# Recurrence of an RWKV-like layer before two expert layers: the mask, the token's own term and the scaled keys move between GpSimd, ScalarE, VectorE and TensorE

## The chip, the cores and the metric

The kernel runs on one core of one Trainium2 chip. The metric is the device time of one execution in microseconds. Before the change the median of three runs is 642.01 us (641.26 to 642.4).

## The reference, cut to what matters

```python
def _attn_ref(r, k, v, w, u):          # r, k, v: [4, 8, 768, 48]; w in 0.85 to 0.95; u: [8, 48]
    for t in range(S):
        cur = u * kt outer vt                       # the token's own term
        y[:, :, t] = rt . (state + cur)
        state = w * state + kt outer vt             # per batch and head: 48 x 48
def reference(...):
    x = attention output as [3072 tokens, 384]
    x = _moe_ref(x)      # tokens with a positive skip score: x + gate * expert(x); 8 experts, 384 -> 1024 -> 384
    return _moe2_ref(x)  # gate * expert(x) of the second layer
```

The time step loop is a recurrence per head; each token is then sent to one of eight experts in each of two layers. All is float32.

## The kernel before, in words

**Recurrence.** The 3072 tokens are 24 tiles of 128, six tiles for each of four batches; a tile has an even half (64 tokens) and an odd half. For a tile `n`, with powers of `w` in the tables TR, TK and TKH, the kernel makes the following pieces, each by a small function inside `attention()`:

- `prep_a`: KTL, the keys times TK (L530, on GpSimd), and XE, the queries times TR (L532, on VectorE), both [112 x 512]: the 48 channels of the odd half at partitions 0 to 47 and those of the even half at 64 to 111. `prep_b` copies the odd half's queries to XO on ScalarE.
- `amat`: TensorE multiplies keys and queries of a half into `a_ps` (L575, L576; 16 products, each of which stands twice in the trace, as two passes of float32). ScalarE copies the result back to XE and XO (L578), and GpSimd zeroes the part in which the key is not before the query, with two `affine_select` (L581).
- `prep_rk` and `prep_kq`: the token's own term. `rkt` = query times key (L547; on GpSimd in 16 tiles, on VectorE in the 8 of RKV), times `u` (L557), summed over the 48 channels of a head into `q` (L562), and `qv` = `q` times the values (L566). In the same function the scaled keys KDE (L560) and KDO (L564) for the state products are made. All of these are VectorE's.
- `uy`: state products `up` (L597, L599) between output products `yp` (L604, L606) on TensorE. ScalarE brings the new state back (L612, L614).
- `finish`: VectorE adds `yp` and `qv` into `xall` (L617), which frees the one bank that `yp` has.

The order on each engine is the order of the code (`manual_schedule`). An iteration `n` of the loop issues: `uy` for the even state of `n` and the odd output of `n-1`; `finish(n-1)`; `prep_a(n+3)`; `amat(n+2)`; `prep_kq(n+2)`; the loads of later tiles, on SyncE (RK for two tiles, `kr` with keys and queries by token, values); `uy` for the odd state and the even output of `n`; `gate_l`, `gate_x` (gate logits of finished tiles, by TensorE); from `n` = 6 on a scatter of a finished tile's rows by GpSimd (L273). `tick` places one operation of the gating of four tiles (`route`) at a time among these.

**Experts.** After the last tile the first expert runs in plain float32, then 16 more jobs of matrix products, in which TensorE is fed from weights that arrive from memory during the job before.

PSUM has eight banks: `a` twice, `y`, `ue`, `uo` in the recurrence, and three for gating.

Of the kernel before, what the change touches and what calls it, by code (L numbers as in the profile page):

```python
# [19 lines left out]
C = 64  # L20
# [23 lines left out]
# slots of a job at which a piece of the next weights is split, and blocks of the next rows are transposed, by the job's row tiles  # L44
# [8 lines left out]
W_LO, W_HI = 0.25, 1.5  # L53
# row tiles that are gated together, by their first: how many, and after how many slots
# [130 lines left out]
def attn_moe_moe_kernel(ctx: ExitStack, tc: tile.TileContext, t, out):  # L185
# [96 lines left out]
    def route(lt, X, g0, n, two, idx_out, ec):  # L282
        """lt: [96, n * 128] parts of the logits; X: row tiles; ec: which first slots.  Yields the engine of the operation to come."""
# [75 lines left out]
    def start(g, lag=0, burst=False, mult=1):  # L359
        """one at a time: they share a bank and the counts"""  # L360
# [5 lines left out]
    def tick(kind, now=False, burst=False):  # L366
        """the next operation of the gating under way if it waits for this engine; after another engine's, some slots later"""
# [37 lines left out]
    def attention():  # L405
        with ExitStack() as actx:
# [6 lines left out]
            u_b = cst.tile([128, DM], F32, name="u_b")  # L413
# [11 lines left out]
            KTL = [cst.tile([128, H, C], F32, name=f"KTL{i}") for i in range(NX)]  # L425
            NL = 3
# [14 lines left out]
            def load_kr(hb):  # L441
                kr[hb] = tok_p.tile([128, LT, 2, DM], F32, tag="kr", bufs=3, name="kr")
                nc.sync.dma_start(out=kr[hb], in_=t["kr"][hb * LT * 128:(hb + 1) * LT * 128].rearrange("(a p) k c -> p a k c", p=128))
# [803 lines left out]
```

## Time and profile before

| | |
|---|---|
| median of 3 runs | 642.01 us |
| span of the profiled execution | 648.0 us |
| recurrence up to the first expert's first product | about 190 us |
| busy: TensorE, VectorE, ScalarE, GpSimd | 87%, 63%, 46%, 46% |
| VectorE in the recurrence | 95% and more of most slices |
| mean granted TensorE clock | 0.928 |

The page names engines PE (TensorE), PEld (its weight loads), DVE (VectorE), ACT (ScalarE), POOL (GpSimd) and SP (SyncE). The times of the profiled execution are about 6 us longer than the median of the runs. The busy share of the whole span mixes the recurrence, in which VectorE hardly rests, with the experts, in which TensorE hardly rests; so stages are read apart.

### The profile page before, as it was taken

What the parts mean: (1) busy time and instruction counts of PE and PEld (TensorE: products, weight loads), DVE (VectorE), ACT (ScalarE), POOL (GpSimd) and SP (SyncE); (2) the same over time, 40 slices, a digit from 0 to 9 for tenths busy, and PEclk for the clock granted to TensorE, in tenths of its full rate; (3) what the DMA queues carried; (4) which work ended last, traced back from release to release, by engine and by line L of the source; (5) the groups of instructions that cost most, each with busy time, mean ns of one, the idle gap of its engine ahead of it and who ended that gap; (6) DMA issues with size and microseconds to landing.
All of it is one profiled execution on the core that took longest, in us unless ns stands there. A gap on an engine that the chain in (4) does not pass through costs nothing. (4 is left out here: it accounts for less than half of the span.)

```text
span 648.0 us, 13115 instructions
## 1 busy us (share of the span) xinstructions
PE 562.8 (87%) x5186; PEld 501.0 (77%) x5188; DVE 405.8 (63%) x732; ACT 295.4 (46%) x584; POOL 298.7 (46%) x312
## 2 busy tenths in 40 slices
PE   5796678778789989999999999997979979699993
PEld 3585566666667888898988999986869868599993
DVE  7998999999725467756676535436454464655320
ACT  5664455564425545554455426443424334254320
POOL 7765585776623175655323224644272524523201
PEclk8877888887979999999999999997998989799997
DMA  8985988679162987676665436342323434333000
GB/s 184 241 203 151 280 213 216 154 171 351 56 220 83 303 277 226 203 243 189 197 183 167 149 105 193 127 148 98 126 79 122 154 105 131 104 127 109 35 13 26
DMA packets 51896, 104.69 MB, mean 162 GB/s; under 512 B 5724, under 2 KB 37592, under 8 KB 51824
## 3 DMA queue, kind: packets, MB, share of 16 engines
q1 hardware_dynamic: 44016, 89.15, 47.7%
q0 software_dynamic: 5904, 11.82, 5.0%
q10 hardware_dynamic: 1904, 2.78, 1.7%
q8 instruction: 43, 0.70, 0.5%
q14 instruction: 29, 0.24, 0.1%
HBM read 82.98 MB, written 26.96 MB: 170 GB/s over the span
## 5 line engine op out<-in xcount | busy, mean ns | idle before, releaser
L1039 PE MATMUL g<-xh,w1h 128*128 128x256 f32 (+3 forms) x384 | 126.4, 329 | 19.1 <-ACT hr L1044 19.1
L1039 PE MATMUL g<-xh,w1l 128*128 128x256 f32 (+3 forms) x384 | 122.8, 320 | 0.0
L1039 PE MATMUL g<-xl,w1h 128*128 128x256 f32 (+3 forms) x384 | 122.4, 319 | 0.0
L1041 DVE SCALAR_TENSOR_TENSOR hl<-g,hh 128x256 fp32r<-128x256 f32 (+1 forms) x128 | 61.2, 480 | 93.1 <-ACT hh L1040 92.5
L1063 PE MATMUL g<-w2h,hh 128*128 128x384 f32 x312 | 109.2, 350 | 0.0
L1063 PE MATMUL g<-w2h,hl 128*128 128x384 f32 x312 | 105.5, 338 | 0.0
L1063 PE MATMUL g<-w2l,hh 128*128 128x384 f32 x312 | 105.2, 337 | 0.0
L1039 PEld LDWEIGHTS g<-xh,w1h 128*128 128x128 f32 x384 | 74.4, 194 | 25.4 <-ACT hr L1044 20.5
L1040 ACT ACTIVATE hh<-g 128x256 fp32r<-128x256 f32 (+1 forms) x128 | 55.1, 430 | 70.1 <-PE g L1039 68.8
L860 POOL TENSOR_TENSOR w1l<-s,w1h 128x1024 fp32r<-128x1024 f32 x14 | 33.4, 2389 | 114.1 <-ACT w1h L859 69.0
L1039 PEld LDWEIGHTS g<-xl,w1h 128*128 128x128 f32 x384 | 74.4, 194 | 1.8 <-DVE xl L1021 0.2
L1039 PEld LDWEIGHTS g<-xh,w1l 128*128 128x128 f32 x384 | 74.2, 193 | 1.6
L860 DVE TENSOR_TENSOR w1l<-s,w1h 128x1024 fp32r<-128x1024 f32 x28 | 57.6, 2056 | 20.9 <-ACT w1h L859 20.9
L273 POOL DMA_INDIRECT xs<-xall,idx_all x48 | 52.3, 1089 | 38.0 <-DVE cum L351 15.9
L273 POOL DMA_INDIRECT out<-rows,ids x30 | 29.2, 973 | 87.3 <-ACT rows L894 62.4
L1063 PEld LDWEIGHTS g<-w2h,hh 128*128 128x128 f32 x312 | 59.3, 190 | 3.1 <-issue 3.0
L1021 DVE TENSOR_TENSOR xl<-xt_ps,xh 128x256 fp32r<-128x256 f32 (+3 forms) x48 | 23.7, 495 | 57.3 <-ACT xh L1020 53.4
L1063 PEld LDWEIGHTS g<-w2l,hh 128*128 128x128 f32 x312 | 58.9, 189 | 0.1
L1063 PEld LDWEIGHTS g<-w2h,hl 128*128 128x128 f32 x312 | 58.5, 188 | 0.0
L606 PE MATMUL yp<-VSE,XE 112*64 112x48 f32 x384 | 31.5, 243 | 26.7 <-DVE xall L617 25.2
L606 PEld LDWEIGHTS yp<-VSE,XE 112*64 112x64 f32 x384 | 28.3, 157 | 28.6 <-DVE xall L617 26.9
L860 DVE TENSOR_TENSOR w2l<-s,w2h 128x1152 fp32r<-128x1152 f32 x28 | 37.9, 1354 | 14.0 <-ACT w2h L859 13.5
(194 smaller groups left out, 1207.2 us busy)
## 6 DMA issues: line engine op xcount, KB each, us to landing
s<-in_w1b SPq DMA_DIRECT2D x24, 512.0 KB
s<-in_w1a SPq DMA_DIRECT2D x21, 512.0 KB
RK<-in_rk SPq DMA_DIRECT2D x24, 384.0 KB
kr<-in_kr SPq DMA_DIRECT2D x12, 768.0 KB
s<-in_w2b SPq DMA_DIRECT2D x16, 576.0 KB
s<-in_w2a SPq DMA_DIRECT2D x14, 576.0 KB
xs<-zrow SPq DMA_DIRECT2D x5, 970.0 KB
VSE<-in_v SPq DMA_DIRECT2D x12, 384.0 KB
```

The costliest lines, as they stand in the source:

```text
L273: i = P.indirect_dma_start(out=dst, out_offset=bass.IndirectOffsetOnAxis(ap=idx_col, axis=0), in_=src, in_offset=None, bounds_check=last, ...
L606: T.matmul(y_ps[ny][0:64, h, 0:D], lhsT=XE[x][0:112, h], rhs=VSE[iy][0:112, jy, h], start=True, stop=True)
L860: (P if j in POOL_LO else V).tensor_tensor(out=lo, in0=x, in1=hi.bitcast(F32), op=ALU.subtract)
L1021: V.tensor_tensor(out=lo, in0=tp[:, 0:cap], in1=hi.bitcast(F32), op=ALU.subtract)
L1039: T.matmul(p, lhsT=a[:, kb, f], rhs=b[:, kb], start=(kb == 0 and i == 0), stop=(kb == KB - 1 and i == 2))
L1040: A.activation(out=hh[:, fb], in_=p[:, 0:full], func=ACTF.Relu)
L1041: V.scalar_tensor_tensor(out=hl[:, fb], in0=p[:, 0:full], scalar=0.0, in1=hh[:, fb].bitcast(F32), op0=ALU.max, op1=ALU.subtract)
L1063: T.matmul(p, lhsT=a[:, fb, r], rhs=b[:, fb], start=(fb == 0 and x == 0), stop=(fb == FB - 1 and x == 2))
```

## The change

Six edits in the recurrence, and what follows from them in other places:

1. KTL is made by VectorE (it was GpSimd's).
2. GpSimd makes one product per tile: RKP = query times key in the channel layout, [112 x 512].
3. TensorE sums the token's own term: 16 products with RKP as the stationary operand and one column of `u` per head as the moving one, into a bank of its own, `q_ps`, right behind the products of `amat`.
4. The mask is a product: VectorE multiplies `a_ps` in PSUM by `before` (ones where the key is before the query) into XE and XO. ScalarE's copies and GpSimd's `affine_select` are gone.
5. `prep_kq` keeps KDE, KDO and `qv`; `qv` reads `q_ps` in PSUM. `rkt`, its product with `u` and the reduction are gone; the queries by token are no longer loaded (`kr` is half as large).
6. `ue` and `uo` become one bank `u`, which pays for the bank of `q_ps`. `u` is loaded by channel (`u_c`, two loads) rather than spread over all partitions. The lower bound on the square of `w` below which the general path is taken rises from 0.25 to 0.7.

```diff
-W_LO, W_HI = 0.25, 1.5
+W_LO, W_HI = 0.7, 1.5
-RKV = (0, 1, 2) + tuple(range(7, NT, 4))
...
-            u_b = cst.tile([128, DM], F32, name="u_b")
+            u_c = cst.tile([112, H], F32, name="u_c")
+            before = cst.tile([128, 1, C], F32, name="before")
...
+            RKP = [cst.tile([112, H, C], F32, name=f"RKP{i}") for i in range(NX)]
...
-                kr[hb] = tok_p.tile([128, LT, 2, DM], F32, tag="kr", bufs=3, name="kr")
+                kr[hb] = tok_p.tile([128, LT, DM], F32, tag="kr", bufs=3, name="kr")
...
+                P.memset(before, 1.0)
+                for r0 in (0, 64):
+                    P.affine_select(out=before[r0:r0 + 64], in_=before[r0:r0 + 64], pattern=[[0, 1], [1, C]], compare_op=ALU.is_gt, fill=0.0, base=0, channel_multiplier=-1)
                 for r0 in (0, 64):
                     nc.sync.dma_start(out=w_c[r0:r0 + D], in_=t["wT"].unsqueeze(2))
+                    nc.sync.dma_start(out=u_c[r0:r0 + D], in_=t["u"].rearrange("(h d) -> d h", d=D))
...
             def prep_a(n):
...
-                P.tensor_tensor(out=kt_[0:112], in0=RK[i][:, 1, j], in1=TK, op=ALU.mult)
+                P.tensor_tensor(out=RKP[x], in0=RK[i][:, 0, j], in1=RK[i][:, 1, j], op=ALU.mult)
+                V.tensor_tensor(out=kt_[0:112], in0=RK[i][:, 1, j], in1=TK, op=ALU.mult)
...
-            def prep_rk(n):
...
             def prep_kq(n):
-                V.tensor_tensor(out=rk, in0=rk, in1=u_b, op=ALU.mult)
                 tick("dve")
                 tick("dve")
...
-                V.tensor_reduce(out=q, in_=rk.rearrange("p (h d) -> p h d", d=D), axis=AX.X, op=ALU.add)
...
-                V.tensor_tensor(out=qv, in0=VSE[hb % NL][:, j], in1=q.to_broadcast([128, H, D]), op=ALU.mult)
+                V.tensor_tensor(out=qv, in0=VSE[hb % NL][:, j], in1=q_ps.pop(n).to_broadcast([128, H, D]), op=ALU.mult)
...
             def amat(n):
...
+                q_ps[n] = ps.tile([128, H, 1], F32, tag="q", name="q_ps")
+                for h in range(H):
+                    for r0, o in ((64, 0), (0, 64)):
+                        T.matmul(q_ps[n][o:o + 64, h], lhsT=RKP[x][r0:r0 + D, h], rhs=u_c[r0:r0 + D, h:h + 1], start=True, stop=True)
                 for X, r0 in ((XE[x], 0), (XO[x], 64)):
-                    A.copy(out=fl(X[r0:r0 + 64]), in_=fl(a_ps[r0:r0 + 64]))
-                # keys before the query; below partition 64 all of the odd buffer stays
-                for X, n_, base in ((XE[x], 64, 0), (XO[x], 128, 64)):
-                    P.affine_select(out=X[0:n_], in_=X[0:n_], pattern=[[0, H], [1, C]], compare_op=ALU.is_gt, fill=0.0, base=base, channel_multiplier=-1)
+                    V.tensor_tensor(out=X[r0:r0 + 64], in0=a_ps[r0:r0 + 64], in1=before[r0:r0 + 64].to_broadcast([64, H, C]), op=ALU.mult)
+                    tick("dve")
...
-                    up = ps.tile([128, H, D], F32, tag="uo" if uodd else "ue", name="up")
+                    up = ps.tile([128, H, D], F32, tag="u", name="up")
...
-            nc.sync.dma_start(out=u_b, in_=t["u"].partition_broadcast(128))
```

**Order on VectorE**, one iteration of the loop without gating in it, from one `finish` (`xall`) to the next; first before, then now. The numbers behind a name are buffers; L532 is L539 in the new numbering, L560 L555, L564 L558, L566 L563, L617 L616.

```order
L617 TENSOR_TENSOR xall<-yp,qv 128x384
L532 TENSOR_TENSOR XE_127<-RK_139,TR 112x512
L557 TENSOR_TENSOR rkt<-rkt,u_b 128x384
L560 TENSOR_TENSOR KDE_122<-kr,TKH 64x384
L562 TENSOR_REDUCE q<-rkt 128x8
L564 TENSOR_TENSOR KDO_125<-kr,TKH 64x384
L566 TENSOR_TENSOR qv<-VSE_141,q 128x384
L617 TENSOR_TENSOR xall<-yp,qv 128x384
```

```order
L616 TENSOR_TENSOR xall<-yp,qv 128x384
L537 TENSOR_TENSOR KTL_136<-RK_144,TK 112x512
L539 TENSOR_TENSOR XE_128<-RK_144,TR 112x512
L579 TENSOR_TENSOR XE_131<-a_ps,before 64x512
L579 TENSOR_TENSOR XO_135<-a_ps,before 64x512
L555 TENSOR_TENSOR KDE_123<-kr,TKH 64x384
L558 TENSOR_TENSOR KDO_126<-kr,TKH 64x384
L563 TENSOR_TENSOR qv<-VSE_146,q_ps 128x384
L616 TENSOR_TENSOR xall<-yp,qv 128x384
```

Two operations are gone between two `finish` (the product with `u` and the reduction), and three are new: KTL ahead of XE, and the two masks, which stand where the product with `u` stood.

**Order on GpSimd**, one iteration in the loop's later part, from one scatter of rows (L273, now L272) to the next; first before, then two iterations now.

```order
L273 DMA xs_76<-xall,idx_all 2048x388
L530 TENSOR_TENSOR KTL_136<-RK_139,TK 112x512
L547 TENSOR_TENSOR rkt<-kr 128x384
L581 AFFINE_SELECT XE_127<-XE_127 64x512
L581 AFFINE_SELECT XO_131<-XO_131 128x512
L273 DMA xs_76<-xall,idx_all 2048x388
```

```order
L272 DMA xs_76<-xall,idx_all 2048x388
L536 TENSOR_TENSOR RKP_141<-RK_144 112x512
L272 DMA xs_76<-xall,idx_all 2048x388
L536 TENSOR_TENSOR RKP_142<-RK_145 112x512
L272 DMA xs_76<-xall,idx_all 2048x388
```

Of four operations between two scatters one is left, and it waits for a load alone, no longer for ScalarE.

**Order on SyncE**, the first loads of the program, which the first operation of the recurrence waits for; first before, then now.

```order
L453 DMA w_c<-in_wT 48x8 x2
L439 DMA RK_139<-in_rk 48x2x1024 x2
L680 DMA RK_139<-in_rk 16x2x1024
L443 DMA kr<-in_kr 128x2x768
L682 DMA u_b<-in_u 128x384
L448 DMA VSE_141<-in_v 128x2x384
```

```order
L458 DMA w_c<-in_wT 48x8
L459 DMA u_c<-in_u 48x8x1
L458 DMA w_c<-in_wT 48x8
L459 DMA u_c<-in_u 48x8x1
L440 DMA RK_144<-in_rk 48x2x1024 x2
L679 DMA RK_144<-in_rk 16x2x1024
L444 DMA kr<-in_kr 128x2x384
L449 DMA VSE_146<-in_v 128x2x384
```

Two loads of `u_c` with single elements now stand ahead of the first RK; `u_b` behind it is gone and `kr` has half the columns.

## Rows read from the trace of the kernel before

**Rows 1.** Busy time by engine in four stretches; the first row names the columns.

```profile
core 0: us, PE busy (x) PEld busy (x) DVE busy (x) ACT busy (x) POOL busy (x), PEclk, DMA share, GB/s
...
32.29:169.04 136.75, 105.61 (x2134) 89.08 (x2134) 132.35 (x212) 74.29 (x149) 87.57 (x118) 0.84 0.79 208
...
189.60:648.00 458.40, 419.87 (x2588) 386.14 (x2585) 238.07 (x434) 196.71 (x388) 177.79 (x144) 0.97 0.46 144
...
13.00:14.00 1.00, 1.00 (x24) 1.00 (x20) 0.97 (x2) 0.96 (x2) 1.00 (x1) 0.50 1.09 184
...
59.85:76.92 17.07, 12.43 (x293) 10.37 (x291) 16.58 (x24) 9.96 (x21) 11.40 (x11) 1.00 1.04 252
```

**Rows 2.** Timeline of VectorE: start us, duration us, engine, line, operation, operands.

```profile
36.15 0.55 DVE L557 TENSOR_TENSOR rkt<-rkt,u_b 128x384 f32<-128x384 f32 x1
36.62 0.54 DVE L560 TENSOR_TENSOR KDE<-kr,TKH 64x384 f32<-64x384 f32 x1
37.09 0.54 DVE L562 TENSOR_REDUCE q<-rkt 128x8 f32<-128x384 f32 x1
37.66 0.56 DVE L564 TENSOR_TENSOR KDO<-kr,TKH 64x384 f32<-64x384 f32 x1
...
39.19 0.68 DVE L532 TENSOR_TENSOR XE<-RK,TR 112x512 f32<-112x512 f32 x1
39.79 0.55 DVE L557 TENSOR_TENSOR rkt<-rkt,u_b 128x384 f32<-128x384 f32 x1
...
62.80 3.24 DVE L564 TENSOR_TENSOR KDO<-kr,TKH 64x384 f32<-64x384 f32 x1
```

**Rows 3.** Timeline of GpSimd beside the last row above.

```profile
62.78 0.65 POOL L581 TENSOR_SCALAR_AFFINE_SELECT XO<-XO 128x512 f32<-128x512 f32 x1
63.41 1.26 POOL L530 TENSOR_TENSOR KTL<-RK,TK 112x512 f32<-112x512 f32 x1
64.63 0.99 POOL L547 TENSOR_TENSOR rkt<-kr 128x384 f32<-128x384 f32 x1
```

**Rows 4.** VectorE's groups in 32.29 to 169 us: busy us, mean ns | idle.

```profile
L564 DVE TENSOR_TENSOR KDO<-kr,TKH 64x384 f32<-64x384 f32 x20 | 33.5, 1677 | 0.6
L532 DVE TENSOR_TENSOR XE<-RK,TR 112x512 f32<-112x512 f32 x20 | 22.1, 1106 | 0.0
L560 DVE TENSOR_TENSOR KDE<-kr,TKH 64x384 f32<-64x384 f32 x20 | 19.4, 971 | 0.0
...
L306 DVE TENSOR_SCALAR eq<-lg 128x4 f32<-128x4 f32 x4 | 2.8, 710 | 0.0
```

**Rows 5.** Two lines of VectorE, whole span: ns min/median/max, first and last start.

```profile
L617 DVE TENSOR_TENSOR xall<-yp,qv x24: 542/550/558, 32.3 to 185.4; 128x384 f32<-128x384 f32 x24
...
L562 DVE TENSOR_REDUCE q<-rkt x24: 533/535/540, 17.7 to 170.6; 128x8 f32<-128x384 f32 x24
```

**Rows 6.** Who waited for whom, 32 to 187 us: total us, times, longest.

```profile
PE yp L606 <- DVE xall L617: 25.2, 12, 6.2
```

**Rows 7.** Timeline of TensorE: around 12 us, and around 60 us.

```profile
12.28 0.37 PE L575 MATMUL a_ps<-XE,KTL 64*64 64x64 f32 x1 [5.20 <-POOL KTL L530]
...
14.18 1.08 PE L512 MATMUL tps<-ident,TH 48*128 48x48 f32 x8
...
60.11 0.27 PE L575 MATMUL a_ps<-XE,KTL 64*64 64x64 f32 x1
...
61.19 0.24 PE L597 MATMUL up<-VSO,KDO 128*48 128x48 f32 x1
...
64.15 0.27 PE L575 MATMUL a_ps<-XE,KTL 64*64 64x64 f32 x1
```

**Rows 8.** Timeline of SyncE's queue: its first issues, with their time.

```profile
0.98 0.88 SPq L453 DMA_DIRECT2D w_c<-in_wT  x2
```

**Rows 9.** Timeline of VectorE: its first wait.

```profile
10.41 0.69 DVE L532 TENSOR_TENSOR XE<-RK,TR 112x512 f32<-112x512 f32 x1 [3.45 <-DMA RK<-in_rk]
```

**Rows 10.** The page, DMA queues: packets, MB, share of 16 engines' span.

```profile
q1 hardware_dynamic: 44016, 89.15, 47.7%
```

More of the change, by code (lines that the diff above doesn't have):

```diff
@@ L441, in load_kr @@
             def load_kr(hb):
-                kr[hb] = tok_p.tile([128, LT, 2, DM], F32, tag="kr", bufs=3, name="kr")
-                nc.sync.dma_start(out=kr[hb], in_=t["kr"][hb * LT * 128:(hb + 1) * LT * 128].rearrange("(a p) k c -> p a k c", p=128))
+                kr[hb] = tok_p.tile([128, LT, DM], F32, tag="kr", bufs=3, name="kr")
+                nc.sync.dma_start(out=kr[hb], in_=t["kr"][hb * LT * 128:(hb + 1) * LT * 128].rearrange("(a p) c -> p a c", p=128))
             def load_v(hb, a=0, b=LT):
@@ L521, in setup5 @@
                     A.copy(out=X[i][r0:r0 + D], in_=X[0][r0:r0 + D])
-            qv_t, q_t, ktil, rk_t = {}, {}, {}, {}
+            ktil, qv_t, q_ps = {}, {}, {}
             def prep_a(n):
@@ L542, in zero_state @@
                 A.copy(out=fl(VSE[n // LT % NL][64:112, n % LT]), in_=warm_src[64:112, 0:DM])
-            def prep_rk(n):
-                hb, j = n // LT, n % LT
-                rk = wk.tile([128, DM], F32, tag="rkt", bufs=3, name="rkt")
-                (V if n in RKV else P).tensor_tensor(out=rk, in0=kr[hb][:, j, 1], in1=kr[hb][:, j, 0], op=ALU.mult)
-                rk_t[n] = rk
             def prep_kq(n):
@@ L553, in prep_kq @@
                 b = n % NB
-                rk = rk_t.pop(n)
-                q = wk.tile([128, H, 1], F32, tag="q", name="q")
-                qv = wk.tile([128, H, D], F32, tag="qv", bufs=3, name="qv")
-                V.tensor_tensor(out=rk, in0=rk, in1=u_b, op=ALU.mult)
+                V.tensor_tensor(out=fl(KDE[b][0:64]), in0=kr[hb][0:64, j], in1=TKH[0:64], op=ALU.mult)
                 tick("dve")
                 tick("dve")
-                V.tensor_tensor(out=fl(KDE[b][0:64]), in0=kr[hb][0:64, j, 0], in1=TKH[0:64], op=ALU.mult)
+                V.tensor_tensor(out=fl(KDO[b][64:128]), in0=kr[hb][64:128, j], in1=TKH[64:128], op=ALU.mult)
                 tick("dve")
-                V.tensor_reduce(out=q, in_=rk.rearrange("p (h d) -> p h d", d=D), axis=AX.X, op=ALU.add)
                 tick("dve")
-                V.tensor_tensor(out=fl(KDO[b][64:128]), in0=kr[hb][64:128, j, 0], in1=TKH[64:128], op=ALU.mult)
-                tick("dve")
-                V.tensor_tensor(out=qv, in0=VSE[hb % NL][:, j], in1=q.to_broadcast([128, H, D]), op=ALU.mult)
+                qv = wk.tile([128, H, D], F32, tag="qv", bufs=3, name="qv")
+                V.tensor_tensor(out=qv, in0=VSE[hb % NL][:, j], in1=q_ps.pop(n).to_broadcast([128, H, D]), op=ALU.mult)
                 tick("dve")
@@ L703, in attention @@
             prep_v(0)
-            prep_rk(0)
             prep_kq(0)
@@ L711, in attention @@
             prep_b(2)
-            prep_rk(1)
             prep_kq(1)
-            prep_rk(2)
             load_rk(2)
@@ L735, in attention @@
                     prep_a(n + 3)
-                    prep_rk(n + 3)
                 tick("dve")
@@ L783, in bank @@
             def bank(tag):
-                return ps.tile([128, H, D], F32, tag=tag, name="f_ps").rearrange("p h d -> p (h d)")
+                return ps.tile([128, H, D], F32, tag=tag, bufs=2 if tag == "a" else 1, name="f_ps").rearrange("p h d -> p (h d)")
             uy(None, 1, NT - 1, 0)
@@ L798, in attention @@
             gate_l(NT - 2)
-            first_T(bank("uo"), (0, 1), 0, CAPA)
-            first_T(bank("ue"), (2,), 0, CAPA)
+            first_T(bank("u"), (0, 1), 0, CAPA)
+            first_T(bank("a"), (2,), 0, CAPA)
             gate_x(NT - 1)
```

2 lines of the change are left out of this document (1 added, 1 removed).

## The prediction

> **What bounds the kernel now.** I read the stretches first. Between the first and the last of 20 equal steps of the recurrence, 32.29 to 169.04 us, VectorE is busy for 132.35 of 136.75 us, GpSimd for 87.57 and TensorE for 105.61 at a granted clock of 0.84; after 189.6 us TensorE takes over, busy for 419.87 of 458.40 us at 0.97 [rows 1]. The list of waits says who holds whom in the recurrence: TensorE's output products wait 25.2 us in 12 waits for VectorE's `finish`, which frees their only bank [rows 6]. So VectorE's list of operations per tile is the step, 136.75 / 20 = 6.84 us.
>
> That list is not slow by its work. In a tile without hindrance one round, from a product with `u` at 36.15 to the next at 39.79, is 3.64 us: `u` 0.47, KDE 0.47, the reduction 0.57, KDO with `qv` and `finish` 1.53, XE 0.60 [rows 2]. Another KDO, the same 64 x 384, takes 3.24 us, from 62.80 to 66.04, while GpSimd runs three operations without a gap from 62.78 to 65.62, which read SBUF [rows 2, 3]. In the groups this is the rule: KDO, XE and KDE take 33.5, 22.1 and 19.4 us for 20 each, where 20 free ones would be 11.2, 13.6 and 10.8; that is 39.4 us of standing still, 1.97 us per step, and even a comparison of four elements averages 0.71 [rows 2, 4]. Two lines never suffer: `finish`, with one input in PSUM, is 0.542 to 0.558 us in all 24 tiles, and the reduction, with one input, 0.533 to 0.540 [rows 5]. So VectorE stands still when it reads two tensors from SBUF while GpSimd works there. The step is 3.64 work + 1.97 standing still of these three + 1.23 rest (gating, the 5 of 20 `rkt` made here, the stalls of short operations, a little idle).
>
> The Trainium skill, page "SBUF — State Buffer", section "Who interferes with whom", has the same division (two SBUF inputs contend with a GpSimd operation that reads SBUF, one does not), but has the lock end with the instruction that holds it. The KDO row differs: it outlasted three. By the page alone one product of GpSimd costs at most its own length; by the rows a queue of them costs its whole length.
>
> **The change part by part.**
>
> VectorE's work. Out: the product with `u`, 0.47, and the reduction, 0.57 [rows 2]. In: KTL, of XE's shape, 0.60, and two masks of 64 x 512. No row shows a mask; it has XE's columns, and a PSUM input costs `finish` nothing (0.55 for 384 columns, as KDE's 0.54 from SBUF), so 0.60 is the lower bound; a change of the starting partition costs 0.1 (the reduction's step ahead of KDO is 0.57 for a duration of 0.54, KDE's 0.47), so 0.78 is the upper bound, XE's whole free duration of 0.68 and that change, nothing overlapped [rows 2, 5]. I take 0.70, XE's step and the change, since steps overlap so in every row. 3.64 - 1.04 + 0.60 + 1.40 = 4.60 us. The rest, 1.23, loses 0.12 (5 x 0.47 / 20) and most of the short operations' stalls; I take 0.75, between 0.6 and 1.1. Without GpSimd: 5.35.
>
> GpSimd's share. Of KTL 1.26, `rkt` 0.99 and two selections of 0.65, 3.55 us per tile, one product of KTL's kind is left, 1.26 [rows 3]. Before, 3.55 us of it held the three long operations for 1.97, a ratio of 0.55; applied to 1.26 that is 0.70. Lower bound nothing, if the product always falls beside the masks, `qv` or `finish`, which now all have one input in PSUM (4 of 8 operations); upper bound its own length, 1.26, since a scatter now stands between two products. I take 0.75. Step: 5.35 + 0.75 = 6.10, against 6.84; 20 steps: -14.8 us. With all lower ends 4.40 + 0.6 + 0 = 5.0, with all upper ones 4.76 + 1.1 + 1.26 = 7.1: -37 to +5 us; the low end is cut by TensorE, next.
>
> TensorE. Around 60 us, at a clock of 1.00, a whole tile went through without a wait from 60.11 to 64.15: 4.04 us, of which the 32 passes of `amat` are 1.08 [rows 1, 7]. The 16 new products are 32 passes too, with the same 48 or 64 rows and 64 columns of weights but one moving column where `amat` has 64. No row has them. Below, half of `amat`, 0.5 us, if only the loads count; above, `amat` at half clock, 14.18 - 12.28 = 1.9 [rows 1, 7]. I take 0.93, near `amat`, because the weights are the same size. TensorE then needs 5.0 and some 0.4 for hand-overs, 5.4 per tile at full clock: it stays behind VectorE's 6.1, with little room. The wait of `q_ps` for the last `qv` (one bank) holds TensorE until just before `finish`, for which the next output products wait anyway; behind it in TensorE's queue stand these first. The state's one bank adds nothing: the odd product reads the even state's copy, and so waits for it already.
>
> ScalarE loses two copies per tile; it was busy for 74.29 of 136.75 us [rows 1], and what they fed is used two tiles later: nothing. As for loads, 4.7 MB of `kr` go; DMA was at a share of 0.79 in this stretch [rows 1] and no wait of VectorE's for it is in it: nothing.
>
> At the start VectorE waits for RK until 10.41 [rows 9]. Ahead of it now stand two loads of `u_c` of 384 single elements each. At the issue they cost 2 x 0.44, as `w_c` [rows 8]; a packet in the main queue takes 0.477 x 16 x 648 / 44016 = 0.112 us of one engine [rows 10], so 768 of them over 16 engines 5.4 us at most. I take +1.3, near the issue's row. From 10.41 to the first `finish`, 21.9 us later [rows 5, 9], four KTL and six masks come, 2.4 + 4.2, and three products with `u`, reductions and `rkt` go, 3 x 1.51: +2.1 of work. At the step's prices three tiles and a fourth XE with their tables are some 13 us of work, an estimate, so 9 stood still; with one product of GpSimd per tile rather than four I take half of that back, -4.5, and give 0.4 for the first scaled keys, which now wait for TensorE's sums at half clock. That is -2.0, with the load -0.7, and 3 either way.
>
> After 169 us, VectorE no longer sets the step, and after 189.6 TensorE, 92% busy, sets the time [rows 1]: what the recurrence saves moves all that follows ahead unchanged.
>
> The sum: -14.8 - 0.7 = -15.5: 648.0 becomes 632.5 in the profile. The median of the runs is 6.0 below the profile's span; the same difference gives **626.5 us**.
>
> **The rivals.**
>
> Nearly no standing still (faster still). For it: RKP waits only for its load, and four of eight operations of VectorE no longer fight it. Then VectorE needs 5.35 and TensorE's 5.4 is the step: 20 x 1.44 = -28.8 and the start's -0.7: 612.5. Against it: KTL with XE, and KDE with KDO, are still 2.2 us of two-input work per step, and GpSimd is freer to meet them.
>
> TensorE at a mixed clock (a smaller gain). Its clock was 0.84 in this stretch; if it stays there and the new products cost `amat`'s 1.08, (4.04 + 1.08) / 0.84 + 0.4 = 6.5 per step: -6.8 and -0.7, 634.5. For it: VectorE's stalls leave gaps, after which the rows at half clock come. Against: fuller work; at 60 to 77 us, with 12.43 of 17.07 busy, it was 1.00 [rows 1].
>
> The new products cost full price on TensorE (slower). Place: between `amat` and the next output products, in every tile. Price: `amat`'s half-clock 1.9 us; at the clock of 0.84, (4.04 + 1.9) / 0.84 + 0.4 = 7.5 per step, 20 x 0.63 = +12.6, with the start 654. It decides against the change from (4.04 + x) / 0.84 + 0.4 = 6.84 on, so x = 1.37 us, 43 ns per pass. For it: 32 more loads of weights for one column each. Against: `amat`, with the same weights, needs 34 ns per pass at full clock. The Trainium skill, "TensorE: Matmul & The Clock Gate", section "LDWEIGHTS (loading the stationary operand)", speaks for this rival: a load costs its columns / 1.2 ns, however few columns move; for 64 that is 53 ns, an estimate of 1.7 us for 32 in a row. `amat`'s passes, 34 ns apart, show loads that overlap between the two halves of the array, and I expect the same here.
>
> The lock stays what it was (no change). If VectorE's long pairs meet GpSimd's product every time, the step is 5.35 + 1.26 + 0.2 = 6.8: 642 with the start. For it: the KDO row, which stood for the whole of what GpSimd had. Against: that was three operations of 2.90 us, now it is one of 1.26 with a scatter behind it [rows 3].
>
> That the general path is taken does not happen: `w` is at least 0.85, its square 0.7225, above the new bound.
>
> **How the numbers follow.** Forecast 0.48 (621 to 632); nearly no standing still 0.22 (607 to 619); mixed clock 0.11; full price 0.11; the lock as before 0.08, of which a third on either side and a third within 0.2%, which is about what a measurement of this kernel can tell from no change. Faster: 0.48 + 0.22 + 0.11 + 0.03 = 0.84, rounded down to 0.83; same 0.03, rounded up to 0.04; slower 0.11 + 0.03, 0.13 after that. The range leaves out the full price and the lowest part of the second case: 610 to 641.
>
> **What would show it.** Right: KDO, KDE, XE and KTL near 0.55 to 0.7 us in the median with outliers of at most some 1.9, masks and `qv` never stretched, 20 steps in about 122 us, RKP alone on GpSimd at 1.3, 32 `q_ps` passes in about 0.9 us, TensorE's waits for `finish` shorter. Wrong: masks over 1 us, or stretched; `q_ps` passes over 43 ns apart with VectorE waiting for TensorE at `finish`; RK's first load landing after 14 us; outliers of 3 us on VectorE as before.

## The result, and the profile after

The changed kernel takes 650.46 us (median of 4 runs, 646.81 to 651.38) against 641.63 of the kernel before beside it: ratio 1.0128, 95% interval 1.0093 to 1.0163. Slower by 1.3%, where 2.4% faster was forecast. Twice more it was 1.0159 (1.0092 to 1.0226) and 1.0148 (1.0109 to 1.0188). The kernel before took 640 to 642 us on some chips and 648 to 649 on others, so all that follows goes by ratios of runs on one chip.

The stretches of the changed kernel are 20 steps from the first `finish`, a stretch at half clock, and the experts; they answer to [rows 1].

```profile
core 0: us, PE busy (x) PEld busy (x) DVE busy (x) ACT busy (x) POOL busy (x), PEclk, DMA share, GB/s
35.96:174.56 138.60, 124.61 (x2781) 109.36 (x2783) 116.29 (x226) 51.75 (x108) 37.68 (x30) 0.83 0.71 176
155.70:169.40 13.70, 13.30 (x191) 10.96 (x190) 9.33 (x23) 4.58 (x11) 2.31 (x2) 0.50 0.90 301
190.00:648.30 458.30, 418.35 (x2583) 384.99 (x2582) 236.73 (x431) 196.83 (x387) 179.05 (x145) 0.97 0.47 146
```

20 steps take 138.60 us, not the 122 forecast and not less than the 136.75 of before. VectorE, which had been busy for 132.35 us of them, is busy for 116.29; TensorE went from 105.61 to 124.61 at the same clock. The two engines have changed places. The second row is the longest stretch at half clock (1.2 GHz) behind the first `finish`; TensorE hardly rests in it. The third row, the experts, is as before. The list of waits, which answers to [rows 6], says so too (who waited for whom: us in total, times, longest):

```profile
DVE xall L616 <- PE yp L603: 23.3, 12, 4.2
...
PE up L598 <- ACT VSE L611: 3.1, 2, 1.7
PE q_ps L577 <- issue: 2.4, 2, 1.6
PE a_ps L572 <- issue: 2.3, 2, 1.9
PE up L598 <- issue: 2.2, 1, 2.2
```

The output products' wait for `finish`, 25.2 us before, is gone from TensorE's list; `finish` now waits 23.3 us for the output products. VectorE's groups in 36 to 174.6 us (busy us, mean ns | idle), against [rows 4]:

```profile
L537 DVE TENSOR_TENSOR KTL<-RK,TK 112x512 f32<-112x512 f32 x20 | 16.0, 802 | 0.0
L555 DVE TENSOR_TENSOR KDE<-kr,TKH 64x384 f32<-64x384 f32 x20 | 15.5, 773 | 0.2
L539 DVE TENSOR_TENSOR XE<-RK,TR 112x512 f32<-112x512 f32 x20 | 14.7, 736 | 0.0
L558 DVE TENSOR_TENSOR KDO<-kr,TKH 64x384 f32<-64x384 f32 x20 | 14.1, 703 | 0.3
L579 DVE TENSOR_TENSOR XO<-a_ps,before 64x512 f32<-64x512 f32 x20 | 13.9, 695 | 0.3
L579 DVE TENSOR_TENSOR XE<-a_ps,before 64x512 f32<-64x512 f32 x20 | 13.4, 670 | 0.7 <-PE a_ps L573 0.6
L616 DVE TENSOR_TENSOR xall<-yp,qv 128x384 f32<-128x384 f32 x21 | 11.6, 553 | 19.7 <-PE yp L603 19.7
```

With free durations (0.68, 0.54, 0.68 and 0.56 us, [rows 2]) the first four groups, with two inputs from SBUF, would be 49.2 us; they are 60.3, so 11 us of standing still are left of 39.4, although KTL has joined them. TensorE's timeline (start, duration, operands, count, idle before) has the new products once with a hole, then at half clock (73.29), then at full clock (81.84):

```profile
37.37 0.23 PE L577 MATMUL q_ps<-u_c,RKP 48*64 48x1 f32 x4
39.15 1.31 PE L577 MATMUL q_ps<-u_c,RKP 48*64 48x1 f32 x28 [1.55 <-issue]
...
73.29 1.82 PE L577 MATMUL q_ps<-u_c,RKP 48*64 48x1 f32 x32
75.03 0.32 PE L596 MATMUL up<-VSO,KDO 128*48 128x48 f32 x1
...
81.84 1.05 PE L577 MATMUL q_ps<-u_c,RKP 48*64 48x1 f32 x32
82.81 0.24 PE L596 MATMUL up<-VSO,KDO 128*48 128x48 f32 x1
```

From their start to the start of the next product the 32 passes cost 0.97 us at full clock and 1.74 at half, that is 0.557 times the speed.

**TensorE's account.** With that ratio the time between two `finish` can be split. In each microsecond TensorE's busy time and granted clock are read. Busy time at full clock is work; busy time at half clock counts 0.557 as work and 0.443 as loss; the rest of the time is waits. For the first 20 steps, in us (one profile each; in profiles of one kernel work repeats within 2.3 us, loss and waits within some 6; the kernels of the lower rows come in the experiments):

| kernel | first finish | 20 steps | work | loss to half clock | waits | last finish | ratio to before |
|---|---|---|---|---|---|---|---|
| before | 32.3 | 136.8 | 87.8 | 17.8 | 31.1 | 185.4 | 1 |
| before, second profile | 33.0 | 136.8 | 86.5 | 18.4 | 31.9 | 186.3 | |
| changed | 36.0 | 138.6 | 104.0 | 20.7 | 13.9 | 186.4 | 1.013 |
| changed, two more profiles | 36.3, 35.6 | 138.7, 142.7 | 104.7, 104.4 | 17.8, 18.1 | 16.2, 20.2 | 193.9, 189.9 | 1.016, 1.015 |
| one head's products | 32.5 | 121.8 | 91.9 | 5.9 | 24.0 | 170.3 | 0.984 |
| the same, second profile | 33.2 | 120.8 | 91.3 | 8.9 | 20.6 | 165.1 | 0.981 |
| before with the products | 34.5 | 144.4 | 103.7 | 20.6 | 20.1 | 189.8 | 1.019 |
| `u` loaded late | 34.9 | 135.3 | 104.6 | 12.9 | 17.8 | 188.9 | 1.012 |
| 64 moving columns | 35.3 | 133.8 | 106.0 | 8.6 | 19.1 | 187.7 | 1.011 |
| keys loaded twice | 35.4 | 147.6 | 105.2 | 19.8 | 22.6 | 199.5 | 1.023 |
| 4 products | 34.9 | 129.0 | 106.7 | 9.7 | 12.6 | 175.1 | 0.996 |
| 4 products, gating later | 35.0 | 127.9 | 108.9 | 8.5 | 10.5 | 173.8 | 0.998 |
| the same, second profile | 35.1 | 129.4 | 106.6 | 14.4 | 8.3 | 176.4 | 0.996 |
| 8 products | 33.4 | 136.4 | 94.1 | 26.4 | 15.9 | 187.9 | 1.000 |
| 8 products, gating later | 32.7 | 132.1 | 98.9 | 21.0 | 12.2 | 181.1 | 0.998 |
| 8, 64 columns, gating later | 33.6 | 129.3 | 98.0 | 13.5 | 17.8 | 173.7 | 0.995 |
| the same, sums in PSUM, `u` late | 35.7 | 127.1 | 98.4 | 8.9 | 19.8 | 173.5 | 0.991 |

From the last `finish` to the end it is 460 to 466 us in every kernel, so the recurrence decides. Of the 31.1 us that TensorE waited before, 25.2 were for `finish`; this was all the room it had. The change used it up and 1.9 us more: 16.2 us of new work, 2.9 of loss, and 8.0 of waits that are not for `finish` (13.9 against 5.9).

**Two kinds of chip.** The three steps behind these 20 took 10.7 to 11.9 us in every profile from a chip on which before takes 640 to 642 us, and 16.0 to 18.8 us in every one from a chip on which it takes 648 to 649, whatever the kernel. By this the profile of before (16.4 us) is from the second kind of chip and the first one of the changed kernel (11.8 us) from the first kind, and their spans, 648.0 and 648.3 us, are not to be compared. On the second kind the changed kernel's span was 657.3 us, 9.3 more than before: 4.0 of it up to the first `finish`, 2.0 in the 20 steps, 2.4 in the next three, 0.8 behind them. In those three steps the 32 passes run through in the changed kernel's first profile (first row), and come in groups in its second (the other rows):

```profile
175.34 1.05 PE L577 MATMUL q_ps<-u_c,RKP 48*64 48x1 f32 x32
```

```profile
175.92 0.89 PE L577 MATMUL q_ps<-u_c,RKP 48*64 48x1 f32 x22
177.22 0.32 PE L577 MATMUL q_ps<-u_c,RKP 48*64 48x1 f32 x5 [0.41 <-issue]
177.93 0.31 PE L577 MATMUL q_ps<-u_c,RKP 48*64 48x1 f32 x5 [0.39 <-issue]
```

### The profile page after: what moved, and what is told of

It is laid out like the page before. It is cut to its first block, busy times and chain, and to the rows that moved or that the text cites. A ratio compares the mean times of both kernels' runs of the same rounds, so it can differ in the third digit from the quotient of the medians.

```text
span 648.3 us, 14513 instructions
## 1 busy us (share of the span) xinstructions
PE 582.4 (90%) x5954; PEld 523.5 (81%) x5956; DVE 386.3 (60%) x748; ACT 269.2 (42%) x536; POOL 242.4 (37%) x251
## 5 line engine op out<-in xcount | busy, mean ns | idle before, releaser
L1057 PE MATMUL g<-w2l,hh 128*128 128x384 f32 x312 | 105.2, 337 | 0.0
L1033 PEld LDWEIGHTS g<-xh,w1h 128*128 128x128 f32 x384 | 74.5, 194 | 25.5 <-ACT hr L1038 20.6
L272 POOL DMA_INDIRECT xs<-xall,idx_all x48 | 50.9, 1060 | 79.0 <-DVE idx_all L348 18.5
L272 POOL DMA_INDIRECT out<-rows,ids x30 | 29.2, 973 | 87.4 <-ACT rows L888 62.7
L536 POOL TENSOR_TENSOR RKP<-RK 112x512 f32<-112x512 f32 x24 | 32.7, 1369 | 63.3 <-DMA RK<-in_rk 60.8
L854 DVE TENSOR_TENSOR w2l<-s,w2h 128x1152 fp32r<-128x1152 f32 x28 | 37.9, 1354 | 14.4 <-ACT w2h L853 14.4
L1014 ACT CAST xh<-xt_ps 128x256 fp32r<-128x256 f32 (+3 forms) x48 | 20.8, 432 | 56.3 <-PE xt_ps L1011 55.8
```

What stands on the lines that cost most here:

```text
L272: i = P.indirect_dma_start(out=dst, out_offset=bass.IndirectOffsetOnAxis(ap=idx_col, axis=0), in_=src, in_offset=None, bounds_check=last, ...
L536: P.tensor_tensor(out=RKP[x], in0=RK[i][:, 0, j], in1=RK[i][:, 1, j], op=ALU.mult)
L854: (P if j in POOL_LO else V).tensor_tensor(out=lo, in0=x, in1=hi.bitcast(F32), op=ALU.subtract)
L1014: A.copy(out=hi, in_=tp[:, 0:cap])
L1033: T.matmul(p, lhsT=a[:, kb, f], rhs=b[:, kb], start=(kb == 0 and i == 0), stop=(kb == KB - 1 and i == 2))
L1057: T.matmul(p, lhsT=a[:, fb, r], rhs=b[:, fb], start=(fb == 0 and x == 0), stop=(fb == FB - 1 and x == 2))
```

## The experiments

**The kernel before once more.**

> The kernel before, unchanged, for a second profile, since the first execution that was profiled had a span of 648.0 us where the median of the runs is 641 to 642. If VectorE's standing still differs from one execution to another, this profile is some 8 us shorter and the outliers of KDO, KDE and XE in 32 to 169 us sum to some 30 us rather than 39.4. If instead TensorE's half clock differs, those sums are the same and the granted clock between the first and the last finish is above 0.84.

The span is 650.3 us on a chip where the runs had a median of 648.43. The stretch and the waits are:

```profile
33.03:169.78 136.75, 104.90 (x2102) 88.65 (x2104) 130.73 (x212) 73.14 (x146) 90.16 (x119) 0.83 0.78 208
```

```profile
PE yp L606 <- DVE xall L617: 23.9, 11, 5.3
...
PE rk L341 <- issue: 1.4, 1, 1.4
```

The same 136.75 us and clock, with less standing still (KDO 29.3, XE 21.4, KDE 18.5 us in the groups, 33.6 above the free durations, against 39.4). Neither reason explains the 6 us between profile and median. They are those of another chip: here, too, the three steps behind the 20 took 16.5 us.

**One head's products only.**

```diff
-                for h in range(H):
+                for h in range(1):
...
-                V.tensor_tensor(..., in1=q_ps.pop(n).to_broadcast([128, H, D]), ...)
+                V.tensor_tensor(..., in1=q_ps.pop(n)[:, 0:1].to_broadcast([128, H, D]), ...)
```

> The changed kernel with the own-term products of one head only (2 products, 4 passes per tile instead of 32); the other seven heads take that head's sum, so that part of the output is left out and all of VectorE's and GpSimd's work stays. Theory A (the passes themselves are the cost, 0.97 us per tile at full clock and 1.74 at half, 28 of 32 of them gone): 24 x 0.85 to 24 x 1.5 off a TensorE that is waited for, about half of it on the path: 650 becomes 630 to 640. Theory B (the passes also keep TensorE at half clock for longer, and their 768 extra matrix instructions run its instruction supply dry): more than the passes' own time comes back, the granted clock between first and last finish rises from 0.82 to 0.9 or more and the finish waits of 23.3 us fall below 8: 615 to 630. Rival C (VectorE's list with KTL and two masks, or the single bank of the state, is the step): no change, 647 to 651.

Seven heads take the first head's sum, so seven heads' own term is left out. The ratio is 0.9838 (0.9786 to 0.989). Once more, on another chip:

> The kernel with one head's products once more, beside the others of this call (seven heads' own term is left out). Its first profile was at a mean clock of 0.949, its other executions at 0.926 to 0.931 and 3 to 6 us longer; 0.98 to 0.985 against before again, and in this profile a loss to half clock of 10 to 20 us rather than 7.4.

It is 0.9812 (0.976 to 0.9865), with a loss of 8.9 us, less than I expected. Stretch and VectorE's wait in the first profile:

```profile
32.45:154.28 121.83, 97.79 (x2243) 84.42 (x2244) 116.40 (x228) 52.14 (x109) 39.91 (x43) 0.94 0.82 203
```

```profile
DVE xall L616 <- PE yp L603: 6.8, 4, 3.2
```

VectorE does the same work (116.40 us against 116.29), its wait falls from 23.3 to 6.8, and 20 steps take 121.83 us: 6.09 each. Some 3% of the time, 19 to 22 us, hangs on 28 of 32 passes per tile. Rival C, VectorE's own list or the single bank of the state, is out. The granted clock rose (0.94 here) and `finish` waited less than 8 us, as theory B expected. But the time that came back is about the 20 us that 28 passes in 24 tiles cost at full clock, so theory A, the passes alone, is not ruled out.

**The same products added to before.**

```diff
+                for h in range(H):
+                    for r0, o in ((64, 0), (0, 64)):
+                        T.matmul(a_ps[o:o + 64, h, 0:1], lhsT=kt_[r0:r0 + D, h], rhs=XE[x][r0:r0 + D, h, 0:1], start=True, stop=True)
```

> The kernel before with 16 more products per tile of the same kind as the changed kernel's (48 rows, 64 columns of weights, one moving column), ahead of amat's into places of a_ps that amat then overwrites; nothing else differs and the result is the same. In before, TensorE waits 24 to 25 us for VectorE's finish. If that wait is room (VectorE alone is the step): the 24 x 0.97 to 1.74 us disappear in it, no change within 3 us. If TensorE has no room in before either, since its busy time at the granted clock and its instruction supply already fill most of the step: it gets slower by 10 to 20 us, ratio 1.015 to 1.03, as the changed kernel lost 18.8 us between one head's products and eight heads' (0.984 against 1.013).

Ratio 1.0189 (1.0146 to 1.0231). VectorE's operations are those of before, yet it waits:

```profile
DVE xall L620 <- PE yp L607: 22.8, 11, 4.7
PE yp L609 <- DVE xall L620: 8.6, 4, 5.1
```

The work grows by 16 us, as in the changed kernel, and TensorE is the step. So before had too little room for these passes; alone they cost as much as the whole change, or a little more.

**`u` loaded behind the first values; 64 moving columns.** The second has a table of 64 equal columns of `u` per head.

```diff
-                    nc.sync.dma_start(out=u_c[r0:r0 + D], in_=t["u"].rearrange("(h d) -> d h", d=D))
...
             load_v(0)
+            for r0 in (0, 64):
+                nc.sync.dma_start(out=u_c[r0:r0 + D], in_=t["u"].rearrange("(h d) -> d h", d=D))
...
-                        T.matmul(..., rhs=u_c[r0:r0 + D, h:h + 1], start=True, stop=True)
+                        T.matmul(..., rhs=u_w[r0:r0 + D, h], start=True, stop=True)
```

> The changed kernel with the two loads of u by channel issued behind the first keys, queries and values instead of ahead of the first RK. The first KTL should start at 10.4 us again instead of 12.4. If the start passes this on: the first finish comes 2 us sooner and the time falls by 2 to 4 us. If the delay is hidden by TensorE's half clock at the start (12.4 to 29 us): the first finish stays at 36 and nothing changes within 1 us.

> The changed kernel with 64 equal columns of u per head as the moving operand instead of one (a table of 112 x 8 x 64, filled by ScalarE at the start); the same 32 passes and the same instructions. If a pass is priced by its weight load, the passes cost as before; if by its columns, they cost what amat's 32 do, 0.98 us at full clock against 0.97 and 1.76 at half against 1.74: by work alone no change within 2 us either way. Theory B in its form that one-column passes hold the half clock (155.8 to 169.2 us is a stretch of 13.4 us at half clock in which TensorE never rests, where the kernel before never needed more than 10): the half-clock stretches get shorter, the granted clock between first and last finish goes from 0.82 to 0.88 or more and the time falls by 6 to 15 us. Instruction supply or gaps alone: no change.

On one chip they gave 1.0117 (1.0062 to 1.0172) and 1.0111 (1.0043 to 1.0178): no change from the 1.013 to 1.016 of the changed kernel, which was not run on that chip. Without the loads of `u` ahead of it the first KTL starts at 10.93 instead of 12.40, but the first `finish` only 1.1 us sooner: TensorE is at half clock there and has two sets of the new passes (1.8 us each) to do; with one head's, the first `finish` is at 32.5 as before. The 64 columns did what I expected of the clock: mean 0.936 to 0.946 in four executions against 0.920 to 0.932 with one column on the same chip. They did not do what I expected of the time: 20 steps are 1.5 us shorter than with `u` loaded late, and the median is the same. Against the first profile of the changed kernel the loss fell by 12.1 us, the 20 steps by 4.8, and the waits grew by 5.2; so a loss to half clock is not paid back in full when it goes.

**Keys by token loaded twice.**

```diff
+                kr2 = tok_p.tile([128, LT, DM], F32, tag="kr2", bufs=3, name="kr2")
+                nc.sync.dma_start(out=kr2, in_=t["kr"][hb * LT * 128:(hb + 1) * LT * 128].rearrange("(a p) c -> p a c", p=128))
```

> The changed kernel with every load of keys by token done twice (the second into a tile that nobody reads), so that the 4.7 MB that the change took from the loads are back; no other work. If TensorE's waits without a releaser (7.5 us in the changed kernel, 14.7 with the loads of u moved, 2.2 to 2.9 before) are instructions that arrive late behind data, they grow by some 5 us and the ratio to 1.02. If they come from the number of instructions alone or the loads have room: no change against the changed kernel within 0.3%.

Ratio 1.0228 (1.0162 to 1.0293) against 1.0159 of the changed kernel beside it. The theory that this run is for says that TensorE's next instruction sometimes arrives late, behind data. TensorE's waits that nothing in the profile releases are 18.6 us between first and last `finish` against 13.5 there:

```profile
PE q_ps L579 <- issue: 5.1, 5, 3.2
PE a_ps L574 <- issue: 2.7, 1, 2.7
PE yp L605 <- issue: 2.6, 2, 1.8
PE rk L341 <- issue: 2.2, 1, 2.2
```

This is what the theory of late instructions expects, though the two intervals overlap, and the other profiles of the changed kernel have 7.4 and 14.0 us. For it speak the hole at 39.15, in the midst of 32 equal passes, and the groups of five in the second profile. The page's queue of instructions grew with the change; these rows are of before and of the changed kernel:

```profile
q8 instruction: 43, 0.70, 0.5%
```

```profile
q8 instruction: 49, 0.80, 0.5%
```

That is six packets and 0.1 MB more for 768 passes and their 768 weight loads. But the waits do not go with them. The kernel before with the same products added has the same 49 packets, and 2.6 us of such waits, as before without them (2.3 and 2.8). One head's products need 43 packets, and have 9.5 and 8.3 us; the first row is of the former, the second of the latter:

```profile
PE a_ps L578 <- issue: 1.7, 1, 1.7
```

```profile
PE a_ps L572 <- issue: 5.4, 2, 4.8
```

So the number of instructions alone does not explain these waits; that they are late instructions at all is not shown.

**Fewer passes: 4 products.** Two heads stand side by side as 128 columns of weights, with 112 rows and four moving columns; ScalarE gathers the useful parts of the result.

```diff
-                for h in range(H):
-                    for r0, o in ((64, 0), (0, 64)):
-                        T.matmul(q_ps[n][o:o + 64, h], ...)
+                for p in range(H // 2):
+                    T.matmul(q4[:, p], lhsT=RKP[x][:, 2 * p:2 * p + 2], rhs=u4[:, p], start=True, stop=True)
+                for b in range(2):
+                    for par in range(2):
+                        A.copy(out=q_ps[n][64 * par:64 * par + 64, :, b], in_=q4[64 * b:64 * b + 64, :, b, par])
```

> The changed kernel with 4 products per tile for the own term in place of 16: two heads as 128 columns of weights, all 112 rows (the gap's rows meet zeros), 4 moving columns (two heads by two halves), 8 passes instead of 32; ScalarE gathers the four useful quarters from PSUM into one small tile, which qv reads. All is computed. If the number of passes and instructions is the cost: it comes near the run with one head's products, ratio 0.984 to 0.99 against before. If a pass is priced by its columns of weights (128 against 64, and no two halves of the array side by side): 8 passes cost 0.9 to 1 us as 32 did, ratio 1.005 to 1.013. Rival: ScalarE's four copies stand ahead of its copies of the state and hold them; TensorE's waits for VSE, 4.6 us in the changed kernel, grow to 15 or more, ratio about 1.0.

Ratio 0.9964 (0.9935 to 0.9993). The 8 passes cost as much as the 32, 0.99 us:

```profile
104.80 1.05 PE L578 MATMUL q<-u,RKP 112*128 112x4 f32 x8
105.79 0.24 PE L601 MATMUL up<-VSO,KDO 128*48 128x48 f32 x1
```

So it is 124 ns for a pass of 128 columns, against 30 ns for one of 64. The work stayed (106.7 us); the 9.6 us that the 20 steps lost came out of loss (11.0) and waits (1.3). Two variants have 34 warming products at the start instead of 17 (products that only keep TensorE busy), and ScalarE's gating (`tick("act")`) behind its copy of the odd state:

```diff
-FILL = (17, 11, {0: 2, 1: 2})
+FILL = (34, 11, {0: 2, 1: 2})
...
-                tick("act")
                 if n % LT == 0:
...
                 elif n + 1 < NT:
                     zero_state(n + 1)
+                tick("act")
```

> The same with 34 instead of 17 warming products at the start, so that TensorE works until about 13 us instead of 7.2, when the first keys arrive at 12.4. In all profiles so far TensorE stands still from 7.2 us on and the first 10 to 17 us of the recurrence run at half clock. If the rest ahead of it is the reason, the clock stays at 1.00 from 12 us on, the first finish comes at 28 to 31 us instead of 33, and the time falls by 2 to 5 us against the kernel with 4 products. If VectorE's list sets the start, or the clock falls at the first small products anyway: no change within 1 us.

> The kernel with 4 products, with ScalarE's gating operation placed behind its copy of the odd state instead of ahead of it (in the changed kernel the exponential waits 15.3 us in 5 times for VectorE's gating, and the copy of the state, which TensorE waits for, stands behind it in ScalarE's queue). If this order is worth its waits: TensorE's waits for VSE (10.3 us with one head's products) fall below 5 and the time falls by 2 to 6 us against the kernel with 4 products. If VectorE sets the step there, no change within 1 us.

The ratios are 0.998 (0.9947 to 1.0014) and 0.9984 (0.9956 to 1.0012): nothing either way. With the warming products the clock fell at 15.6 us instead of 12, and the first `finish` stayed at 34.9. The second of the two kernels again, on another chip:

> The kernel with 4 products and ScalarE's gating behind its copy of the state once more, on the chip of the others of this call. If the difference of 0.996 to 1.000 between 4 and 8 products was that of two chips: the same ratio as before the move to another chip would give, 0.998, and not below the kernel with 8 products of an earlier call (0.998 with the same order on ScalarE). If the higher clock that came with 128 columns of weights (loss 8.5 to 9.7 us) is the kernel's own: a mean clock of 0.94 again.

It gave 0.9958 (0.9926 to 0.999). Its executions had mean clocks of 0.932 to 0.949, where before had 0.922 to 0.940 on this chip; its profile had a loss of 14.4 us, where the first profile of this kernel had 8.5.

**Cheaper passes: 8 products.** Each takes one head, all 112 rows and 64 columns of weights; neighbours use the other half of the output partitions.

```diff
+                for h in range(H):
+                    p, b = divmod(h, 2)
+                    T.matmul(q2[64 * b:64 * b + 64, p], lhsT=RKP[x][:, h], rhs=u2[:, h], start=True, stop=True)
```

> Own term by 8 products per tile, one head each: all 112 rows, 64 columns of weights, two moving columns (the two halves), heads alternating between the two halves of the output partitions, so that neighbouring passes use different columns of the array; 16 passes in place of 32 (changed kernel) or of 8 with 128 columns (4 products). ScalarE gathers as with 4 products. All is computed. If a pass costs 30 to 35 ns when its neighbour uses the other half of the array, as the state and output products do (35 ns): 0.5 us per tile instead of 0.97, TensorE's work falls from 116 to 105 to 108 us, and the time to ratio 0.98 to 0.99 against before. If two passes that use the same rows do not overlap (124 ns per pass of 128 columns, so 62 for 64): 1.0 us as in both other kernels, ratio 0.995 to 1.0. Rival: TensorE's price does not matter, only the instruction supply does: as with 4 products, 0.996, or a little worse.

> The same with ScalarE's gating operation behind its copy of the odd state. With 4 products it took TensorE's waits for VSE from 3.0 us to none and moved the time by nothing that could be told (0.9984 against 0.9964, intervals of 0.003). With one head's products these waits were 10.3 us in TensorE's account. If a lighter TensorE waits more for ScalarE: 0.003 to 0.008 below the kernel with 8 products. If VectorE's list is the step by then: no change.

The ratios are 0.9999 (0.9967 to 1.0032) and 0.9981 (0.9949 to 1.0013); 0.98 to 0.99 was expected of the first. The price is as hoped, 0.49 us, 31 ns per pass:

```profile
102.21 0.63 PE L579 MATMUL q<-u,RKP 112*64 112x2 f32 x16
102.70 0.25 PE L611 MATMUL yp<-VSE,XE 112*64 112x48 f32 x1
```

The work falls to 94.1 us and the loss rises to 26.4, at a clock of 0.77: what the passes saved, the clock took. The execution of this profile took 653.86 us, where the median is 649.73; with the gating later the profile has 98.9 us of work and 21.0 of loss. Two tries on that, both with the gating later, take 64 moving columns (32 equal ones per half), and one product of 128 x 512 more per tile:

```diff
-            u2 = cst.tile([112, H, 2], F32, name="u2")
+            u2 = cst.tile([112, H, 2, 32], F32, name="u2")
```

```diff
+                T.matmul(q2.rearrange("p a b -> p (a b)"), lhsT=warm_src[:, 0:128], rhs=warm_src, start=True, stop=True)
```

> Own term by 8 products, ScalarE's gating behind its copy of the state, and 64 moving columns (32 equal ones per half) in place of two; the same 16 passes. If few moving columns hold the half clock: a pass stays near 34 ns, the work near 107 us, and the loss to half clock falls from 24 to 29 us with two columns to some 10, as it was 11.5 with 64 columns in 32 passes: 10 to 15 us faster than with two columns, ratio 0.975 to 0.985 against before. If the clock falls by the gaps ahead of it and not by what the passes carry: ratio 0.998 as with two columns.

> The kernel with 8 products and two moving columns, with one product more per tile ahead of them that only keeps TensorE busy (128 x 512 in one pass, 0.2 to 0.4 us as those at the start, its result overwritten). It adds 5 us of work or more. If the clock answers to what the passes carry: the loss to half clock falls by 10 us or more and the time is the same or up to 8 us lower than without, ratio 0.985 to 0.998. If it does not: the added work shows, ratio 1.004 to 1.01.

The ratios are 0.9953 (0.9926 to 0.998) and 1.0002 (0.9974 to 1.0029). The loss was 13.5 and 15.2 us, but on another chip than with two columns, and neither the 0.975 to 0.985 expected of the first nor the 0.985 to 0.998 of the second came. VectorE had a new price in all kernels with 4 and 8 products so far: `qv` read the gathered sums from SBUF, two inputs beside GpSimd, and took 0.75 to 0.87 us on average. With 64 columns, the sums gathered into PSUM and `u` loaded late:

```diff
-                q_ps[n] = wk.tile([128, H // 2, 2], F32, tag="qs", bufs=3, name="qs")
+                q_ps[n] = qb[:, 256:264].rearrange("p (a b) -> p a b", b=2)
```

> 8 products with 64 moving columns, with the gathered sums written by ScalarE into PSUM, so that qv has one input in PSUM again, and the loads of u behind the first values. If VectorE's list is part of the step (6.47 us against 6.04 with one head's products, where qv read PSUM): 19 x 0.29 = 5.5 us of qv's time go, the step falls to about 6.25 and the time by 3 to 6 us: ratio 0.985 to 0.991 against before. If TensorE's work, half clock and waits are the step (108 + 13 + 18 us between first and last finish): no change, 0.995. Rival: the sums' bank is now held until qv has read it, TensorE's waits for qv (1.4 us) grow by 3 us or more, and the ratio is 0.995 to 1.0.

> The changed kernel unchanged beside it, for a ratio on the same chip. Expected 1.012 to 1.016 against before, as twice so far, and a TensorE account of 116 us of work and 33 to 42 us of half-clock loss and waits.

The ratio is 0.9912 (0.988 to 0.9944), beside 1.0148 of the changed kernel: 636.94 us against 642.22 before and 652.56. `qv` is back at its price. Its bank is waited for, as the rival expected (6.1 us after 1.4), but the ratio is not the rival's 0.995 to 1.0:

```profile
L564 DVE TENSOR_TENSOR qv<-VSE,qb 128x384 f32<-128x384 f32 x19 | 10.5, 554 | 0.6
```

```profile
PE qb L579 <- DVE qv L564: 6.1, 7, 2.1
```

This kernel is faster than both; which of its two edits did it is not told apart. The changed kernel as it is, beside the kernels with 8 products, had this expectation:

> The changed kernel unchanged, on the chip and beside the kernels with fewer products, for a second profile. TensorE's account between the first and the last finish was 116 us of work (its busy time, with that at half clock taken at 0.557), 21 us lost to half clock and 13 us of waits, 7.5 of them with nothing that releases it. Expected: ratio 1.010 to 1.015 against before, the same work within 2 us, and loss and waits together 30 to 38 us, shared differently.

## Why the prediction was wrong, step by step

- **VectorE's side was right.** The masks took 0.64 to 0.70 us and were never stretched, `qv` 0.554 us; KDO, KDE, XE and KTL stood still for 11 us in 20 steps where 15 were taken, and none of them took more than 1.80 us. Where TensorE is not in the way the step is 6.09 and 6.04 us, as the forecast's 6.10.
- **The passes' price was right:** 0.97 us at full clock against 0.93, 1.74 at half against the 1.9 of the bound.
- **The step that failed** is "TensorE then needs 5.0 and some 0.4 for hand-overs, 5.4 per tile at full clock: it stays behind VectorE's 6.1". The work was nearly right, 104.0 / 20 = 5.2 us. But a step holds 1.03 us of loss to half clock, for which the forecast had nothing, and 0.70 of waits: 6.93. The loss stood in [rows 1], as a clock of 0.84; I took the one tile at a clock of 1.00 [rows 7] for the rule. In before it cost little only because TensorE had 25.2 us of waiting for `finish` beside it [rows 6], 1.3 us per step. The new work took 16.2 us of that; more loss and more waits took the rest. That the passes on TensorE are what costs is shown both ways, by taking 28 of 32 out (1.013 to 0.984) and by adding them to before (1.019); how much of it is loss and how much waits is read from the account and was not set one by one. Of the 24.8 us between the forecast's span of 632.5 and the 657.3 us measured on the same kind of chip, these 20 steps are 16.8 and the start is 4.7.
- **The rival "TensorE at a mixed clock" was the right mechanism, priced too low.** Its 6.5 us per step took 0.4 for hand-overs where 0.70 were, and the step's work 0.1 too small; with these, 5.2 / 0.84 + 0.7 = 6.9, no gain. It had a chance of 0.11; with the clock in hand it should have been the forecast. "Full price on TensorE" came to the right side by a price that did not occur: 30 ns per pass at full clock, not 43 or more.
- **VectorE's saving came, and was of no use.** Its busy time got 16 us shorter in 20 steps (132.35 to 116.29 us), and all of it became waiting.
- **The start** was forecast at -0.7 us and cost +3.7 (first `finish` 36.0 against 32.3). The loads of `u` held the first operation for 2.0 us where 1.3 were taken, and moving them brought only 1.1 back; without 28 passes per tile nearly all was gone (32.5 and 33.2). Waits for TensorE's sums at half clock had been given 0.4 us there, where two sets of new passes take 1.8 us each.
- **Behind the last `finish`** nothing changed, as forecast: 461.9 against 462.6 us (460 to 466 in all kernels).
- **The median** taken 6 us under the profile's span was a difference between chips; the runs lie 1.7 us above their spans (650.0 and 648.3). It did no harm, as only the saving counted.

What stays open: what holds the clock at half (the loss was 12.9 to 26.4 us in kernels with 32 or 16 passes of one or two columns, and 17.8 in before, which has none), since profiles of one kernel differ by some 6 us; what the waits without a releaser are; and why the last three steps take 5 to 7 us longer on some chips.

## What to carry to other kernels

Where one engine's list is the step, write the next engine's step as an account before loading it: work, loss at the clock that the stretch really had, and waits that are not for the first engine. Room is only the wait for the first engine. Of small products the layout sets the price: passes of 64 columns whose neighbour uses the other half of the output partitions came four times as close as passes of 128 columns over the full width, each of which does the work of two.

## What the runs showed of the hardware that was not expected

- 32 passes of 48 rows x 64 columns take 0.97 us, 16 of 112 x 64 take 0.49, and 8 of 112 x 128 take 0.99: 30, 31 and 124 ns. The Trainium skill, "TensorE: Matmul & The Clock Gate", section "Part 3: Packing small matmuls — row/col tiling", lets a weight load overlap a running product only where the row group differs. The 112-row passes use the same rows and are 31 ns apart, so here the measurement decides: different halves of the columns are enough. Passes of 64 columns that all use the same half were not run.
- The clock may take back a saving: the kernels with 8 products of two columns and nothing added had 8 to 15 us less work than those with 4, and 7 to 18 us more of loss, on different chips.
- The chips of this case differ most in one place: the three steps behind the 20 took 10.7 to 11.9 us on some and 16.0 to 18.8 on others, whatever the kernel.
